# GpSimd in place of VectorE for the four combined weight blocks of the mixer, behind the scatters of the last slots

## The chip, the cores and the metric

One core of one Trainium2 chip runs the whole program. The metric is device time in microseconds of one execution: median of 3 runs 1476.76 us (1476.22 to 1486.14). The profiled execution is one of its own and took 1480.18 us, with a span of 1478.5 us from the first to the last instruction.

## The reference

Three stages follow one another on 8 sequences of 576 tokens of 512 values (4,608 tokens).

```
attention   softmax over chunks of 64 keys, 8 heads of 64
experts     logits = x @ w_gate (8 experts); a sigmoid gate lets a token keep the expert of the token before
            out[b,s] = p[e] * (relu(x[b,s] @ w1[e]) @ w2[e])          w1: 512x1024, w2: 1024x512
mixer       u  = x + (x^T @ U @ V)^T                                   rank 32 across the 576 positions
            out = u + relu(u @ w_ch1) @ w_ch2                          512 -> 2048 -> 512
```

All inputs are float32. The kernel multiplies float16 pairs (a high half and the rest) and gets float32 accuracy from three products.

## The kernel before

**Stages.** Attention takes the first 210 us. The expert stage follows, up to about 722 us: the tokens are sorted by expert, and 128 of them at a time make a slot. The mixer takes the rest, to 1478 us, and is carried by TensorE.

**A slot.** The order of all work is written out by hand, and every engine takes its instructions strictly in that order. In the round of slot `t` (loop at L1429) TensorE computes layer 1 of slot `t+2` (L907), transposes the hidden rows of slot `t+1` (L960), and computes layer 2 of slot `t` (L975). ScalarE rectifies (L952), makes high halves (L965, L869), and copies the result of layer 2 into `ysb` (L982), which has one buffer. VectorE makes the low halves (L966, L870). GpSimd then scatters the rows of `ysb` to their tokens in the DRAM tensor `yd` (L788, an indirect DMA). A scatter waits for the DMA of the write to `yd` before it. From slot 33 on (`NM - 9`, with `NM` = 42) up to two scatters of a zero tile follow the scatter of each slot (L1476), 11 in all; the last one belongs to slot 38. Rounds 36 to 41 are the last six; a round lasts 11.2 us.

**Combined weights.** The mixer's second product uses a scheme with seven block products, whose weights are sums and differences of the blocks of `w_ch2`. Half of these combined blocks are made early by GpSimd in `sums_piece` and kept in DRAM. The other four (index 2, 3, 0, 1) are made by `combine` (L1066) in the rounds 36 to 40. I call the two parts of `combine` its head and its tail. The head is one addition of 128x768 (L1072, float16 in, float32 out) and four subtractions of 128x256 (L1080), and is put at the end of rounds 36, 37, 38 and 39, behind their scatters. The tail stands at the end of the next round: ScalarE makes the high half `th` (L1075, 128x1024) from the head's result, and one subtraction of 128x1024 makes the low half `tl` (L1076). So the order at the end of a round is: scatter of the slot, scatters of zero, tail of the block before, head of the next block.

**Into the mixer.** The mixer's preparation is a list `steps`. Step 0, `load_x` for five pieces (L1205, DMAs issued by SyncE), stands in round 39 ahead of layer 2; it reads `yd`, and so stands behind the scatter of slot 38 and the last zero scatter. Steps 1 to 5, `emit_x`, stand at the start of round 40's layer 2: ScalarE makes a high half (L1236), VectorE a low half (L1230). The next steps stand inside the second layers of slots 40 and 41: `emit_t` (TensorE, L1244 and L1247), `emit_u` (L1267, L1269, L1270), `emit_sa` and `emit_sb` (GpSimd L1296, L1302, L1313, L1314; ScalarE L1299, L1306; VectorE L1230; transposing DMAs L1292 of rows `row1`, `row2`, and of `row3`, which shares its memory with `row1`). The scatter of slot 40 and the tail of block 1 stand at the end of round 40, ahead of `emit_sa`. The first mixer product (L1523) reads what these DMAs bring.

Of the kernel before, what the change touches and what calls it, by code (L numbers as in the profile page):

```python
# [13 lines left out]
ALU = mybir.AluOpType  # L14
# [26 lines left out]
def chunk_attention__moe__mixer_kernel(  # L41
# [15 lines left out]
    nc = tc.nc  # L57
# [33 lines left out]
    bh, bl = (t[:, :HC * 3 * HD].rearrange("p (c o n) -> p c o n", c=HC, o=3) for t in c2)  # L91
    b12 = [t[:, HC * 3 * HD:].bitcast(F32).rearrange("p (c n) -> p c n", n=HD) for t in c2]
# [402 lines left out]
    with tc.manual_schedule():  # L495
# [7 lines left out]
            out=tri, in_=ones, pattern=[[-1, 128]], compare_op=ALU.is_ge, fill=0.0, base=0, channel_multiplier=1  # L503
# [14 lines left out]
        for b in range(B):  # L518
# [23 lines left out]
            out=wg_l, in0=wg_raw, scalar=S_WG, in1=wg_h, op0=ALU.mult, op1=ALU.subtract  # L542
# [512 lines left out]
    th, tl = [], []  # L1055
# [10 lines left out]
    def combine(c):  # L1066
        bf, t = (
            m_p.tile([128, 512, 2], F32, tag="raw64", name="raw64").rearrange("p a b -> p (a b)") for _ in range(2)
        )
        bf = bf[:, :3 * HD].rearrange("p (o n) -> p o n", o=3)  # L1070
        t = t.rearrange("p (o n) -> p o n", o=4)
        nc.vector.tensor_tensor(out=bf, in0=bh[:, c], in1=bl[:, c], op=ALU.add)  # L1072
        sums(nc.vector, t, bf[:, 0], b12[0][:, c], bf[:, 1], bf[:, 2])
        yield
        nc.scalar.activation(out=th[c], in_=t, func=AF.Copy)  # L1075
        nc.vector.tensor_tensor(out=tl[c], in0=t, in1=th[c], op=ALU.subtract)  # L1076

    def sums(engine, t, b11, b12, b21, b22):
        for n, x, y in ((0, b12, b11), (2, b22, b12), (1, b22, t[:, 0]), (3, b21, t[:, 1])):
            engine.tensor_tensor(out=t[:, n], in0=x, in1=y, op=ALU.subtract)  # L1080
# [289 lines left out]
    with tc.manual_schedule():  # L1370
# [58 lines left out]
        for t in range(EN, NM):  # L1429
# [48 lines left out]
            if NM - 6 <= t < NM - 2:  # L1478

                combined = combine((2, 3, 0, 1)[t - NM + 6])  # L1480
                next(combined)
# [242 lines left out]
```

## Time and profile before

| quantity | value |
|---|---|
| median of 3 runs | 1476.76 us |
| profiled execution, and its span | 1480.18 us, 1478.5 us |
| TensorE matmul busy | 1355.0 us, 92% of the span |
| VectorE busy | 1086.6 us, 73% |
| ScalarE busy | 761.6 us, 52% |
| GpSimd busy | 624.9 us, 42% |
| chain that ended last, by engine | PE 58%, DVE 14%, DMA 11%, ACT 5%, issue 5%, POOL 3% |

PE is TensorE, DVE is VectorE, ACT is ScalarE, POOL is GpSimd, SP is SyncE. The shares are means over three stages with different limits. What a change in the rounds 36 to 41 is worth is to be read from the stretch of 660 to 740 us.

### The profile page before, as it was taken

The page shows a single profiled execution, that of the slowest core. Times are in us where ns is not written, and L with a number is a line of the kernel's source. Part 1 is how long each engine was busy: PE and PEld are TensorE (multiplying, and loading weights), DVE is VectorE, ACT ScalarE, POOL GpSimd, SP SyncE. Part 2 cuts the span into 40 slices and gives each one's busy share as a digit, 9 for nine tenths or more (in the row PEclk, how much of TensorE's full clock was granted, in tenths as well). Part 3 has the DMA queues.
Part 4 walks back from the last instruction along what each step waited for, and adds up shares of the span by engine and source line. Part 5 has one row for each costly group of instructions (what it writes and reads, how often), then busy time and mean ns, then how long its engine had stood idle before and what let it go on. Part 6 is the DMA issues. An engine that isn't in the chain of part 4 may idle for free.

```text
span 1478.5 us, 33713 instructions
## 1 busy us (share of the span) xinstructions
PE 1355.0 (92%) x12070; PEld 988.3 (67%) x12070; DVE 1086.6 (73%) x1740; ACT 761.6 (52%) x1158; POOL 624.9 (42%) x640
## 2 busy tenths in 40 slices
PE   7687888899999999999679999999999999999995
PEld 5676763444544544545357888888878888888884
DVE  5677767477777777767567778778778788877772
ACT  5566851466666666665344444444444444444441
POOL 2356322125767766533233334434434443443331
PEclk9889998999999999999999999999999999999998
DMA  8879873888569788532486778777788887877873
GB/s 200 210 211 213 203 181 76 269 222 205 130 187 238 175 235 252 134 76 63 138 195 123 148 151 167 159 145 165 154 164 157 158 161 137 166 147 140 141 131 83
DMA packets 513342, 244.27 MB, mean 165 GB/s; under 512 B 429652, under 2 KB 472660, under 8 KB 512916
## 3 DMA queue, kind: packets, MB, share of 16 engines
q1 hardware_dynamic: 505572, 223.14, 68.1%
q0 software_dynamic: 7600, 18.89, 4.6%
q8 instruction: 104, 1.70, 0.5%
q14 instruction: 66, 0.54, 0.1%
HBM read 163.96 MB, written 39.19 MB: 137 GB/s over the span
## 4 chain that ended last, share of the span: by engine, by line
PE 58%; DVE 14%; DMA 11%; ACT 5%; issue 5%; POOL 3%; SPq 2%; DVEq 0%; another core or an unknown queue 0%; ACTq 0%; POOLq 0%
PE y L975 14%; PE o L1585 13%; PE h L907 13%; PE a L1523 12%; DMA c<-in_q_dram 3%; POOL r L1556 3%; PE m L960 2%; DMA w1l<-c 2%; DMA w1h<-c 2%; DVE hn L1566 2%; ACT hn L1565 2%; ACT r L1552 1%; DVE pre L1548 1%; DVE pre L1551 1%; DMA hT<-hn 1%
## 5 line engine op out<-in xcount | busy, mean ns | idle before, releaser
L1556 POOL TENSOR_TENSOR r<-r 128x256 f32<-128x256 f32 x216 | 222.8, 1032 | 439.0 <-ACT r L1552 427.7
L1585 PEld LDWEIGHTS <-hT 128*128 128x128 f16 x3024 | 296.8, 98 | 52.2 <-issue 9.5
L975 PE MATMUL y<-w2h,hT 128*128 (+1 forms) x672 | 208.8, 383 | 0.1
L1566 DVE TENSOR_TENSOR hn<-r,hn 128x768 f16<-128x768 f32 (+1 forms) x144 | 171.5, 1191 | 33.7 <-ACT hn L1565 33.7
L1552 ACT ACTIVATE r<-pre 128x1024 f32<-128x1024 f32 x72 | 76.1, 1057 | 221.1 <-DVE pre L1551 221.1
L1523 PEld LDWEIGHTS <-w1h 128*128 128x128 f16 x1512 | 148.2, 99 | 47.3 <-DMA w1h<-c 17.5
L975 PEld LDWEIGHTS <-hT 128*128 128x128 f16 x1008 | 99.2, 99 | 114.2 <-issue 6.0
L1523 PEld LDWEIGHTS <-w1l 128*128 128x128 f16 x1512 | 147.0, 98 | 36.6 <-DMA w1l<-c 15.1
L1585 PE MATMUL o<-c,hT 128*128 128x256 f16 x1296 | 166.5, 274 | 4.0 <-DMA hT<-hn 3.7
L907 PE MATMUL h<-w1h,xT 128*128 (+1 forms) x624 | 166.3, 379 | 1.9 <-ACT h L952 1.9
L907 PEld LDWEIGHTS <-xT 128*128 128x128 f16 x936 | 91.5, 98 | 112.1 <-DMA xT<-xs 1.4
L1565 ACT ACTIVATE hn<-r 128x768 f16<-128x768 f32 (+1 forms) x144 | 136.6, 949 | 39.5 <-POOL r L1556 34.3
L788 POOL DMA_INDIRECT yd<-ysb,idx x39 | 61.5, 1577 | 162.6 <-ACT ysb L982 106.5
L975 PE MATMUL y<-w2l,hT 128*128 (+1 forms) x336 | 128.5, 382 | 0.0
L1523 PE MATMUL a<-c1h,w1h 128*128 128x256 f16 x576 | 114.0, 276 | 4.3 <-DMA w1h<-c 2.9
L966 DVE TENSOR_TENSOR hT<-m,hT 128x512 f16<-128x512 f32 x78 | 50.2, 687 | 88.6 <-ACT hT L965 88.6
L1523 PE MATMUL a<-c1h,w1l 128*128 128x256 f16 x576 | 112.0, 273 | 0.0
L870 DVE SCALAR_TENSOR_TENSOR w1l<-w1s,w1h 128x1024 f32 (+1 forms) x76 | 93.4, 1265 | 24.3 <-ACT w1h L869 22.6
L1585 PE MATMUL o<-w2s,hT 128*128 128x256 f16 x864 | 107.1, 274 | 0.0
L1585 PE MATMUL o<-w1s,hT 128*128 128x256 f16 x864 | 106.7, 273 | 0.0
L907 PE MATMUL h<-w1l,xT 128*128 (+1 forms) x312 | 92.8, 379 | 0.0
L870 DVE SCALAR_TENSOR_TENSOR w2l<-w2s,w2h 128x1024 f32 (+1 forms) x76 | 90.1, 1227 | 2.6 <-ACT w2h L869 1.2
(318 smaller groups left out, 2563.0 us busy)
## 6 DMA issues: line engine op xcount, KB each, us to landing
w1s<-in_moe_w_dram SPq DMA_DIRECT2D x38, 1024.0 KB
w2s<-in_moe_w_dram SPq DMA_DIRECT2D x38, 1024.0 KB
raw<-in_moe_w_ch_dram SPq DMA_DIRECT2D x32, 512.0 KB
c1h<-in_v_dram SPq DMA_DIRECT2D x144, 64.0 KB
xd<-xhl SPq DMA_DIRECT2D x36, 256.0 KB
w1l<-yd SPq DMA_DIRECT2D x28, 256.0 KB
c<-in_q_dram SPq DMA_DIRECT2D x12, 512.0 KB
c<-in_k_dram SPq DMA_DIRECT2D x12, 512.0 KB
```

Source lines behind the costliest of these rows:

```text
L788: nc.gpsimd.indirect_dma_start(out=yd, out_offset=bass.IndirectOffsetOnAxis(ap=at, axis=0), in_=y, in_offset=None, bounds_check=NT - 1, oo ...
L870: nc.vector.scalar_tensor_tensor(out=l, in0=x, scalar=scale, in1=h, op0=ALU.mult, op1=ALU.subtract)
L907: nc.tensor.matmul(out=ps[g], lhsT=x[:, a, :], rhs=w(kk, slice(g * 512, g * 512 + 512)), start=(i == 0 and j == 0), stop=(i == KD - 1 and ...
L960: nc.tensor.transpose(out=ps[g][:, a], in_=h[:, g, a], identity=ident)
L966: nc.vector.tensor_tensor(out=hT[:, g, 1], in0=ps, in1=hT[:, g, 0], op=ALU.subtract)
L975: nc.tensor.matmul(out=ps, lhsT=hT[:, f // 4, a, f % 4], rhs=w(f, slice(0, DM)), start=(i == 0 and j == 0), stop=(i == KF - 1 and j == 2),)
L1523: nc.tensor.matmul(out=out if len(z.shape) == 2 else out.rearrange("p (g n) -> p g n", n=128), lhsT=u[:, u_at(a, x, kk)], rhs=z, start=(fi ...
L1552: nc.scalar.activation(out=r[:, 0:4], in_=pre, func=AF.Relu)
L1556: nc.gpsimd.tensor_tensor(out=r[:, o], in0=r[:, x], in1=r[:, y], op=op)
L1565: nc.scalar.activation(out=row3[:, 0], in_=x, func=AF.Copy)
L1566: nc.vector.tensor_tensor(out=row3[:, 1], in0=x, in1=row3[:, 0], op=ALU.subtract)
L1585: nc.tensor.matmul(out=y if len(z.shape) == 2 else y.rearrange("p (g n) -> p g n", n=128), lhsT=hT[:, h_at(a, x, c2)], rhs=z,  start=(c == ...
```

## The change

The five instructions of the head and the subtraction of the tail are issued by GpSimd. Nothing is moved in the written order, so they stand in GpSimd's queue behind the scatters of their rounds. ScalarE's `th` stays.

```diff
@@ def combine(c):
-        nc.vector.tensor_tensor(out=bf, in0=bh[:, c], in1=bl[:, c], op=ALU.add)
-        sums(nc.vector, t, bf[:, 0], b12[0][:, c], bf[:, 1], bf[:, 2])
+        nc.gpsimd.tensor_tensor(out=bf, in0=bh[:, c], in1=bl[:, c], op=ALU.add)
+        sums(nc.gpsimd, t, bf[:, 0], b12[0][:, c], bf[:, 1], bf[:, 2])
         yield
         nc.scalar.activation(out=th[c], in_=t, func=AF.Copy)
-        nc.vector.tensor_tensor(out=tl[c], in0=t, in1=th[c], op=ALU.subtract)
+        nc.gpsimd.tensor_tensor(out=tl[c], in0=t, in1=th[c], op=ALU.subtract)
```

`sums` issues the four subtractions on the engine that it is given:

```
    def sums(engine, t, b11, b12, b21, b22):
        for n, x, y in ((0, b12, b11), (2, b22, b12), (1, b22, t[:, 0]), (3, b21, t[:, 1])):
            engine.tensor_tensor(out=t[:, n], in0=x, in1=y, op=ALU.subtract)
```

## Rows read from the trace of the kernel before

**Rows 1.** The page's first line, for the whole execution.
```profile
span 1478.5 us, 33713 instructions
```

**Rows 2.** Busy time by stretch: length, then each engine's busy us, clock, DMA.
```profile
690.00:700.00 10.00, 10.00 (x52) 5.00 (x50) 6.03 (x10) 5.35 (x8) 2.07 (x2) 1.00 0.33 103
700.00:710.00 10.00, 6.14 (x29) 3.07 (x28) 8.90 (x14) 5.71 (x10) 0.97 (x1) 0.94 0.20 69
```

**Rows 3.** The chain that ended last, 690 to 735: start us, length, what.
```profile
690.04 5.18 PE h L907 x24
...
698.12 4.54 DMA w1l<-yd
...
722.51 4.22 DMA w1h<-c
...
726.84 0.64 ACT c L1306
```

**Rows 4.** GpSimd in order of time: start us, length, instruction, [idle before, releaser].
```profile
677.12 1.71 POOL L788 DMA_INDIRECT yd<-zero,idx  x1 [2.90 <-DMA yd<-zero,idx]
...
684.56 1.86 POOL L788 DMA_INDIRECT yd<-zero,idx  x1 [2.01 <-DMA yd<-ysb,idx]
687.77 0.97 POOL L788 DMA_INDIRECT yd<-zero,idx  x1 [1.36 <-DMA yd<-zero,idx]
691.00 0.97 POOL L788 DMA_INDIRECT yd<-ysb,idx  x1 [2.25 <-ACT ysb L982]
694.01 1.10 POOL L788 DMA_INDIRECT yd<-zero,idx  x1 [2.03 <-DMA yd<-ysb,idx]
703.44 0.97 POOL L788 DMA_INDIRECT yd<-ysb,idx  x1 [8.34 <-ACT hT L965]
717.90 1.17 POOL L788 DMA_INDIRECT yd<-ysb,idx  x1 [13.49 <-ACT ysb L982]
719.66 1.42 POOL L1296 TENSOR_TENSOR w2h<-w1h 128x256 f32<-128x256 f32 x1 [0.59 <-PE y L975]
...
724.48 0.72 POOL L1314 TENSOR_TENSOR w2h<-w1h 128x256 f32<-128x256 f32 x1
```

**Rows 5.** Waits of SyncE's DMA queue, 640 to 760: total us, times, longest.
```profile
SPq L1205 <- DMA yd<-zero,idx: 5.8, 1, 5.8
```

**Rows 6.** SyncE's issues in order of time: the first loads of the mixer.
```profile
696.27 1.80 SPq L1205 DMA_DIRECT2D w1h<-yd  x4
```

**Rows 7.** ScalarE in order of time, rounds 37, 38 and 40.
```profile
679.39 1.05 ACT L1075 ACTIVATE w1s<-raw 128x1024 f16<-128x1024 f32 x1
680.34 2.16 ACT L869 ACTIVATE w1h<-w1s 128x1024 f32 x2
...
703.76 1.95 ACT L1236 ACTIVATE w1l<-w1h,psel 128x512 f16<-128x512 f32 x3
```

**Rows 8.** VectorE in order of time, at both ends of round 40.
```profile
703.91 1.22 DVE L1076 TENSOR_TENSOR w1s<-raw,w1s 128x1024 f16<-128x1024 f32 x1
705.05 0.95 DVE L1072 TENSOR_TENSOR raw<-c,c 128x768 f32<-128x768 f16 x1
...
707.51 2.73 DVE L1230 SCALAR_TENSOR_TENSOR w1l<-w1h,psel,w1l 128x512 f16<-128x512 f32 x4
...
719.27 1.22 DVE L1076 TENSOR_TENSOR w1s<-raw,w1s 128x1024 f16<-128x1024 f32 x1
```

**Rows 9.** TensorE in order of time: `emit_t`, and layer 2 behind it.
```profile
708.31 0.38 PE L1247 MATMUL m<-w1l,uA 128*96 128x512 f16 x1 [3.39 <-DVE w1l L1230]
...
712.16 0.39 PE L975 MATMUL y<-w2h,hT 128*128 x1
```

**Rows 10.** GpSimd's lines of like operations: ns min/median/max, first and last start us.
```profile
L1108 POOL TENSOR_TENSOR sums<-c,c x8: 902/905/1892, 527.8 to 606.3; 128x384 f32<-128x384 f16 x8
...
L1302 POOL TENSOR_TENSOR w2h<-w2h,w1h x12: 727/731/1052, 721.2 to 1349.7; 128x256 f32<-128x256 f32 x12
...
L590 POOL TENSOR_TENSOR w1l<-w1s,w1h x4: 2128/2132/2136, 68.1 to 104.2; 128x1024 f16<-128x1024 f32 x4
```

## The prediction

> **What bounds it now.** I read the page first, then busy time by stretch around the change, then the chain that ended last, then each engine in order of time. The span is 1478.5 us [rows 1]; the profiled execution took 1480.18 us, 3.4 us above the median of the runs, 1476.76. Up to slot 39's second layer TensorE has no gap: 10.00 of 10 us busy; in the next 10 us it is busy for 6.14 [rows 2]. So what VectorE does in rounds 36 to 38 is hidden already, and only the passage into the mixer, from about 697 to 731 us, is set by something else. The reader should see two strands in it. One is the data: the loads of the mixer's input wait for the last zero scatter [rows 5], start at 696.27 [rows 6] and land at 698.12 + 4.54 = 702.66 [rows 3]. The other is VectorE: at 703.91 it makes a tail, at 705.05 a head, and only from 707.51 the low halves [rows 8] for which TensorE has idled 3.39 us at 708.31 [rows 9]. This second strand is what the change takes off. GpSimd looks free, with 8.34 and 13.49 us of idle time ahead of the scatters of slots 39 and 40 [rows 4]; but its queue carries the scatters on which the first strand hangs, and it runs strictly in order.
>
> **Prices.** No row shows this 128x768 addition on GpSimd. The nearest, 128x384 of the same types, takes 0.905 us, at most 1.892; twice that is 1.8 to 3.8, and I take 1.8, since the median is nearly the minimum. A subtraction of 128x256 takes 0.73. So a head costs 1.8 + 4 x 0.73 = 4.7 us, against 707.51 - 705.05 = 2.5 on VectorE [rows 8]. The tail has its shape in a row: 2.13 [rows 10], against 1.22. GpSimd gets 4 x (4.7 + 2.1) = 27 us more; VectorE loses 15.
>
> **Meetings.** GpSimd's 128x256 addition at 719.66 takes 1.42 [rows 4] where its like takes 0.73: VectorE's subtraction of two SBUF operands ran until 719.27 + 1.22 = 720.49 [rows 8], and the excess is what was left of it. So where the two meet, one waits for the other. An instruction on GpSimd loses between 0 and 1.22 us by it, a VectorE instruction between 0 and 2.13 (behind a tail). The Trainium skill (SBUF — State Buffer, section "Who interferes with whom") says more: the shared ports are locked for a whole instruction, and the later engine fully blocks. This row agrees with it; with a lock the sum below is 5.5 us, with evenly shared ports it would be about 4.5.
>
> **The queue, step by step.** Four heads and four tails stand in GpSimd's order; nothing in the order of the DMAs changes, but each is issued later.
> Head 2 starts when slot 36's second zero scatter ends, 677.12 + 1.71 = 678.83, and ends at 683.6. Only then come slot 37's scatter (0.2 us of issue, 0.97) and its zeros after 2.01 and 1.36 us of DMA wait [rows 4], up to 690.1. Tail 2, with 0.7 for a meeting, and head 3 last from there to 697.8. Slot 38's scatter is issued at 698.1 instead of 691.00, so 7.1 late, and the last zero scatter, 3.01 behind it as now, at 701.1 instead of 694.01. The loads of the mixer's input start at 703.4 and land at 709.8, again 7.1 late.
> Behind the zero scatter come tail 3 (702.3 to 704.4) and head 0, with another 0.7, to 709.9. ScalarE's `th` of block 0 cannot start before it, and lasts 1.05 [rows 7]; behind it in ScalarE's order stands `emit_x`, which so starts at 711.1 instead of 703.76: 7.3 late. This is the added wait; queued behind it are all of ScalarE's high halves, and VectorE and TensorE wait for those.
> Here VectorE's relief comes back. Its low halves no longer stand behind a tail and a head; the first follows its high half by 0.7, at 711.8 instead of 707.51, 4.3 late. But tail 0 is released by the same `th` and meets them: up to 2.1 more, and I take it whole, because it is issued first. The low halves, `emit_t` and the rest of layer 2, which resumes at 712.16 now [rows 9], are then some 6 us late, and so is slot 40's scatter, 717.90 now.
> Head 1 is done by then (about 719.5 against 723.9). Tail 1 stands between that scatter and `emit_sa`: 2.1 more for L1296, less the 0.7 that it lost to VectorE's tail, so L1314 ends 6 + 1.4 = about 7 us later than 725.2 [rows 4], at 732.2. The transposition of `row1` gains the 1.2 of VectorE's tail and lands 4.8 late, at 726.73 + 4.8 = 731.5 (722.51 + 4.22 now). ScalarE's 726.84 step needs both [rows 3], and goes to 732.3: **5.5 us late.** From there the mixer has the same work, and I see nothing that gives a late start back.
>
> **What stays covered.** `th` of blocks 2 and 3 also wait for their heads. Block 2's moves from 679.39 to 683.6 and pushes ScalarE's weight halves from 680.34 to 684.6 [rows 7]; with VectorE's half they are ready by about 688, and TensorE needs them in the middle of the layer that runs from 690.04 to 695.22 [rows 3], 4.6 us later. If a head took 9.3 us, that cover would be gone. Tensor work of slot 40 is held up by 2 to 4 us through block 3's `th`, but `emit_x` comes later still, so it adds nothing.
>
> **The sum.** Without any meeting the result is 5.5 - 0.7 - 0.7 - 2.1 = 2.0 us late; with one more lock of 1.22 in each of tail 2, head 3, tail 3 and head 0 it is some 10. On the profiled execution: 1480.18 + 5.5 = 1485.7, with 1482 to 1490. On the median of the runs: 1482.3, with 1478.8 to 1486.8. About 1%, 14.8 us, is what a measurement can tell here, so this counts as no change.
>
> **Rivals.**
> *The queue absorbs it.* GpSimd has 8.34 and 13.49 us of idle time there and is busy 42% of the whole. If the loads do not hang on the late scatters, or heads cost near VectorE's 2.5, only the relief is left: the first low half follows `emit_x` at 703.76 by 0.7 + 0.7, and TensorE's 708.31 becomes about 705.1. That gives -3.2: 1473.6. Against it: SyncE's wait names the zero scatter [rows 5], and the idle time lies behind the heads, not where they stand. 0.16.
> *A lock in nearly every instruction.* Heads 2, 3 and 0 stand one behind the other on the path; each microsecond more in a head counts three times. By the worst of rows 4 and 10 a head is 3.8 + 4 x 1.42 = 9.5 and a tail 2.13 + 1.22 = 3.35. Then slot 38's scatter comes at 707.9, the loads land near 719.6, and `emit_x` starts near 726, 22 late; with the relief the end is about 20 late: 1496.8. From heads of 7.8 on the loss passes 1%. Against it: ScalarE stands still while it waits for a head, so VectorE has little to do then, and meetings should be few. 0.08. The lock of the page named above is what would make it.
> *TensorE's wait hides even the late loads*, so that the result is within 2 us of now (1475 to 1479): for it speaks that TensorE already idles there, against it that the wait is filled by the first strand from 702.66 on. It lies between the first rival and the forecast, 0.08.
>
> **Numbers.** Forecast 0.68. Its own range is 1478.8 to 1486.8. To leave out no more than 2 in 10 I go down over half of the first rival, to 1474.5, and up to 1489, which takes in the upper bound of the meetings. Faster by over 1% (under 1462) has no mechanism: 0.02. Slower by over 1% (over 1491.5) is the second rival: 0.08. The rest, 0.90, is within 1%.
>
> **What would show it.** Between slots 36 and 39 GpSimd's rows should show five additions and subtractions after each round's zero scatters, 4.7 to 5.5 us together. Slot 38's scatter should come about 7 us after where it is now, and the first L1205 loads with it. ScalarE should idle ahead of L1075 with the head's last subtraction as releaser. VectorE should have no L1072 and no L1076, and its L1230 should follow L1236 directly. TensorE's gap ahead of L1247 should be longer, not gone, and the first L1523 should start 4 to 7 us later. The prediction is wrong if the loads start near 696 in spite of the late scatters, if heads take under 3 or over 8 us, or if the mixer's own length changes: nothing in it is touched.

## The result and the profile after

The changed kernel is slower: 1492.78 us, median of four runs (1491.46 to 1496.45), against 1476.49 (1474.85 to 1486.14) for the kernel before on the same chip. The ratio is 1.010, 95% interval 1.006 to 1.014, or 9 to 21 us. The profiled executions say 1493.23 and 1480.18 us, 13.05 apart. Forecast were 5.5 us, at most 1489: the sign was right, the size was not. The kernel before ran 17 to 31 times beside each experiment, and its medians there were 1478.15 to 1480.05 us; so part of the 16.3 us between the two medians here may be the luck of four executions.

Where are the 13 us? I measure both traces from ScalarE's copy of slot 37's result (L982), the last event that the change cannot reach, to the first matmul of the mixer's second product (L1585). I call this **the passage**. First the kernel before, ScalarE and then TensorE, then the same two rows after.

```profile
678.89 0.60 ACT L982 ACTIVATE ysb<-y 128x512 f32<-128x512 f32 x1 [1.22 <-issue]
```
```profile
714.76 0.38 PE L1267 MATMUL m<-w1h,vA 128*128 128x512 f16 x1
...
726.78 0.28 PE L1523 MATMUL a<-c1h,w1h 128*128 128x256 f16 x1 [2.90 <-DMA w1h<-c]
...
756.87 2.08 PE L1585 MATMUL o<-c,hT 128*128 128x256 f16 x9 [0.29 <-issue]
```
```profile
678.35 0.60 ACT L982 ACTIVATE ysb<-y 128x512 f32<-128x512 f32 x1 [1.22 <-issue]
```
```profile
712.29 0.59 PE L1244 MATMUL m<-w1l,uA 128*128 128x512 f16 x1 [7.92 <-ACT w1l L1236]
716.14 0.59 PE L1247 MATMUL m<-w1l,uA 128*96 128x512 f16 x1 [3.26 <-DVE w1l L1230]
...
721.17 0.61 PE L975 MATMUL y<-w2h,hT 128*128 x1
...
725.75 0.38 PE L1267 MATMUL m<-w1h,vA 128*128 128x512 f16 x1
...
737.60 0.28 PE L1523 MATMUL a<-c1h,w1h 128*128 128x256 f16 x1 [2.69 <-DMA w1h<-c]
...
768.28 1.14 PE L1585 MATMUL o<-c,hT 128*128 128x256 f16 x9 [0.29 <-issue]
```

The passage went from 756.87 - 678.89 = 77.98 to 768.28 - 678.35 = 89.93 us: 11.95 longer. Ahead of it the execution after is 0.5 us shorter, behind it 1.6 longer; so nearly all of the profiled 13.05 lies here. The stretch behind it varied from 719.2 to 729.1 us over all the executions below, whatever was changed, and that is why each experiment is read by its passage as well as by its runs.

The whole page hides this. GpSimd is busy 44% of the span after:

```profile
span 1491.5 us, 33726 instructions
...
PE 1363.1 (91%) x12070; PEld 992.6 (67%) x12070; DVE 1087.9 (73%) x1716; ACT 761.1 (51%) x1158; POOL 652.2 (44%) x664
```

GpSimd in order of time says more; it answers to [rows 4]. From one slot's scatter to the next, 682.93 to 697.97, its queue needs 15.04 us, and the only idle times in it are the waits for the scatters' DMAs. A round lasted about 11.2 us before.

```profile
682.93 1.00 POOL L788 DMA_INDIRECT yd<-ysb,idx  x1 [0.15 <-issue]
685.94 0.98 POOL L788 DMA_INDIRECT yd<-zero,idx  x1 [2.01 <-DMA yd<-ysb,idx]
688.28 0.97 POOL L788 DMA_INDIRECT yd<-zero,idx  x1 [1.35 <-DMA yd<-zero,idx]
689.26 2.14 POOL L1076 TENSOR_TENSOR w1s<-raw,w1s 128x1024 f16<-128x1024 f32 x1
691.35 1.65 POOL L1072 TENSOR_TENSOR raw<-c,c 128x768 f32<-128x768 f16 x1
693.07 1.60 POOL L1080 TENSOR_TENSOR raw<-c,raw 128x256 f32<-128x256 f32 x1
694.63 1.70 POOL L1080 TENSOR_TENSOR raw<-raw,c 128x256 f32<-128x256 f32 x1
696.30 1.52 POOL L1080 TENSOR_TENSOR raw<-raw,raw 128x256 f32<-128x256 f32 x2
697.97 0.99 POOL L788 DMA_INDIRECT yd<-ysb,idx  x1 [0.15 <-issue]
...
711.78 2.16 POOL L1076 TENSOR_TENSOR w1s<-raw,w1s 128x1024 f16<-128x1024 f32 x1
713.86 1.66 POOL L1072 TENSOR_TENSOR raw<-c,c 128x768 f32<-128x768 f16 x1
715.60 1.06 POOL L1080 TENSOR_TENSOR raw<-c,raw 128x256 f32<-128x256 f32 x1
...
717.76 2.30 POOL L1080 TENSOR_TENSOR raw<-raw,raw 128x256 f32<-128x256 f32 x2
728.90 1.18 POOL L788 DMA_INDIRECT yd<-ysb,idx  x1 [8.84 <-ACT ysb L982]
```

Note the prices: in head 3 (691.35 to 697.82) two of the four subtractions take 1.60 and 1.70, though one alone takes 0.73 [rows 10]; the other two, 1.52 together, are nearly undisturbed. SyncE's wait, the row of [rows 5], is now 7.2 us, and the loads of [rows 6] start at 703.14:

```profile
703.14 1.80 SPq L1205 DMA_DIRECT2D w1h<-yd  x4
```

ScalarE, as in [rows 7]: it idles 6.36 us for head 0, and `emit_x` is right behind that `th`.

```profile
710.57 1.06 ACT L1075 ACTIVATE w1s<-raw 128x1024 f16<-128x1024 f32 x1 [6.36 <-POOL raw L1080]
711.53 2.54 ACT L1236 ACTIVATE w1l<-w1h,psel 128x512 f16<-128x512 f32 x4
```

VectorE, as in [rows 8]. The four low halves that took 2.73 us take 7.20, while GpSimd has tail 0 and then head 1 (711.78 and 713.86 above). The first of the four, shown once more by itself, takes 3.81 of them: it ends 0.56 us after the head's addition.

```profile
688.68 7.07 DVE L870 SCALAR_TENSOR_TENSOR w2l<-w2s,w2h 128x1024 f32 x2
...
708.40 1.27 DVE L966 TENSOR_TENSOR hT<-m,hT 128x512 f16<-128x512 f32 x2
...
712.27 7.20 DVE L1230 SCALAR_TENSOR_TENSOR w1l<-w1h,psel,w1l 128x512 f16<-128x512 f32 x4 [2.60 <-ACT w1l L1236]
719.40 1.20 DVE L1230 SCALAR_TENSOR_TENSOR w1l<-w1l,psel 64x512 f16<-64x512 f32 x1
```
```profile
712.27 3.81 DVE L1230 SCALAR_TENSOR_TENSOR w1l<-w1h,psel,w1l 128x512 f16<-128x512 f32 x1 [2.60 <-ACT w1l L1236]
```

The fifth low half of the kernel before, which ended at 710.89:

```profile
710.16 0.73 DVE L1230 SCALAR_TENSOR_TENSOR w1l<-w1l,psel 64x512 f16<-64x512 f32 x1
```

Last the stretches, as in [rows 2]. TensorE does 3.95 and 4.10 us of work in the two stretches from 700 to 720, and its granted clock in 710 to 720 is 0.50, the lower of its two levels (1.2 GHz); before it was 0.89 in the same stretch.

```profile
690.00:700.00 10.00, 10.00 (x52) 5.08 (x51) 5.75 (x2) 2.33 (x5) 8.66 (x7) 1.00 0.06 20
700.00:710.00 10.00, 3.95 (x21) 1.89 (x20) 9.12 (x6) 4.21 (x7) 8.83 (x7) 0.91 0.40 125
710.00:720.00 10.00, 4.10 (x8) 1.07 (x7) 7.73 (x5) 4.12 (x6) 9.59 (x8) 0.50 0.07 26
```

Lateness against the kernel before, both counted from the L982 copy, in us:

| event | forecast | measured |
|---|---|---|
| slot 38's scatter | 7.1 | 7.5 |
| first loads (L1205) | 7.1 | 7.4 |
| `emit_x` on ScalarE | 7.3 | 8.3 |
| last low half of `emit_x` done | about 6 | 10.25 |
| layer 2 resumes (L975) | 6 | 9.55 |
| slot 40's scatter | 6 | 11.5 |
| first mixer matmul (L1523) | 5.5 | 11.4 |
| first matmul of the second product (L1585) | 5.5 | 11.95 |

The queue was forecast within half a microsecond as far as the loads. The rest is lost between `emit_x` and slot 40's scatter.

### The profile page after: what moved, and what is told of

Read it like the earlier page. It is cut to its first block, busy times and chain, and to the rows that moved or that the text cites. A ratio compares the mean times of both kernels' runs of the same rounds, so it can differ in the third digit from the quotient of the medians.

```text
span 1491.5 us, 33726 instructions
## 1 busy us (share of the span) xinstructions
PE 1363.1 (91%) x12070; PEld 992.6 (67%) x12070; DVE 1087.9 (73%) x1716; ACT 761.1 (51%) x1158; POOL 652.2 (44%) x664
## 4 chain that ended last, share of the span: by engine, by line
PE 47%; DVE 15%; issue 10%; DMA 10%; POOL 9%; ACT 5%; SPq 3%; POOLq 0%; DVEq 0%; ACTq 0%
PE o L1585 13%; PE a L1523 13%; PE y L975 9%; PE h L907 7%; DMA c<-in_q_dram 4%; POOL r L1556 2%; DMA w1h<-c 2%; DVE hn L1566 2%; DMA w1l<-c 2%; ACT hn L1565 2%; ACT r L1552 1%; PE m L960 1%; POOL yd L788 1%; DVE pre L1548 1%; POOL xs L330 1%
## 5 line engine op out<-in xcount | busy, mean ns | idle before, releaser
L1585 PEld LDWEIGHTS <-hT 128*128 128x128 f16 x3024 | 296.3, 98 | 50.8 <-issue 9.3
L975 PE MATMUL y<-w2h,hT 128*128 (+1 forms) x672 | 210.3, 385 | 0.0
L1523 PEld LDWEIGHTS <-w1h 128*128 128x128 f16 x1512 | 149.6, 100 | 46.9 <-DMA w1h<-c 16.7
L975 PEld LDWEIGHTS <-hT 128*128 128x128 f16 x1008 | 99.8, 99 | 115.8 <-issue 8.6
L1523 PEld LDWEIGHTS <-w1l 128*128 128x128 f16 x1512 | 148.3, 99 | 37.7 <-DMA w1l<-c 14.6
L1585 PE MATMUL o<-c,hT 128*128 128x256 f16 x1296 | 165.6, 273 | 3.5 <-DMA hT<-hn 3.2
L975 PE MATMUL y<-w2l,hT 128*128 (+1 forms) x336 | 129.2, 385 | 0.0
L966 DVE TENSOR_TENSOR hT<-m,hT 128x512 f16<-128x512 f32 x78 | 50.2, 686 | 92.7 <-ACT hT L965 92.7
L1523 PE MATMUL a<-c1h,w1h 128*128 128x256 f16 x576 | 114.2, 276 | 2.8 <-DMA w1h<-c 2.7
L870 DVE SCALAR_TENSOR_TENSOR w1l<-w1s,w1h 128x1024 f32 (+1 forms) x76 | 91.6, 1240 | 31.2 <-ACT w1h L869 30.1
L1523 PE MATMUL a<-c1h,w1l 128*128 128x256 f16 x576 | 113.9, 276 | 0.0
L1585 PE MATMUL o<-w2s,hT 128*128 128x256 f16 x864 | 107.3, 274 | 0.0
L1585 PE MATMUL o<-w1s,hT 128*128 128x256 f16 x864 | 106.1, 273 | 0.0
L870 DVE SCALAR_TENSOR_TENSOR w2l<-w2s,w2h 128x1024 f32 (+1 forms) x76 | 100.3, 1361 | 2.0 <-ACT w2h L869 1.2
```

The source lines that it names most:

```text
L870: nc.vector.scalar_tensor_tensor(out=l, in0=x, scalar=scale, in1=h, op0=ALU.mult, op1=ALU.subtract)
L966: nc.vector.tensor_tensor(out=hT[:, g, 1], in0=ps, in1=hT[:, g, 0], op=ALU.subtract)
L975: nc.tensor.matmul(out=ps, lhsT=hT[:, f // 4, a, f % 4], rhs=w(f, slice(0, DM)), start=(i == 0 and j == 0), stop=(i == KF - 1 and j == 2),)
L1523: nc.tensor.matmul(out=out if len(z.shape) == 2 else out.rearrange("p (g n) -> p g n", n=128), lhsT=u[:, u_at(a, x, kk)], rhs=z, start=(fi ...
L1585: nc.tensor.matmul(out=y if len(z.shape) == 2 else y.rearrange("p (g n) -> p g n", n=128), lhsT=hT[:, h_at(a, x, c2)], rhs=z,  start=(c == ...
```

## The experiments

The theory after the result: (a) GpSimd's occupied queue makes the scatters, and with them the loads, late; (b) head 1, not only tail 0, takes turns with the low halves; (c) the longer gap of TensorE costs clock behind it. The rivals: one of these alone is the whole loss, or the late start of the loads is not on the path. Experiments 1 to 5 and 7 edit the changed kernel; 6 and 8 the kernel before; 9 is built on 6.

**1 and 2. Half of the change each.** Only blocks 2 and 3 on GpSimd, or only blocks 0 and 1.

```diff
+        eng = nc.gpsimd if c in (2, 3) else nc.vector     # experiment 2: (0, 1)
-        nc.gpsimd.tensor_tensor(out=bf, in0=bh[:, c], in1=bl[:, c], op=ALU.add)
-        sums(nc.gpsimd, t, bf[:, 0], b12[0][:, c], bf[:, 1], bf[:, 2])
+        eng.tensor_tensor(out=bf, in0=bh[:, c], in1=bl[:, c], op=ALU.add)
+        sums(eng, t, bf[:, 0], b12[0][:, c], bf[:, 1], bf[:, 2])
...
-        nc.gpsimd.tensor_tensor(out=tl[c], in0=t, in1=th[c], op=ALU.subtract)
+        eng.tensor_tensor(out=tl[c], in0=t, in1=th[c], op=ALU.subtract)
```

> Blocks 2 and 3 on GpSimd, blocks 0 and 1 on VectorE as before. Theory: the loss of the change (16.3 us by the medians, 13 by the profiled executions) has three parts. The queue: slot 38's scatter and the mixer's loads come 7 us late because GpSimd needs more per round than the round lasts. The meetings in round 40: tail 0 and head 1 on GpSimd slow VectorE's low halves of emit_x. The clock: TensorE runs at half speed some 4 us longer after the longer gap. Here the first part stays whole: scatter of slot 38 near 698, loads starting near 703 and landing near 709.5. The second is gone, since VectorE makes tail 0 and head 1 while it waits for the loads: the four low halves of emit_x take 2.7 us instead of 7.2. So +3 to +6 us against before. Rival (the loss lies in rounds 36 to 39, where ScalarE and VectorE are slowed by the heads, in proportion to their number): +7 to +9.

Measured for blocks 2 and 3: 1490.14 against 1480.05, ratio 1.0072 (1.0050 to 1.0094), passage 8.76 us longer than before. That is the rival's figure, but not by the rival's cause: `emit_x`'s low halves run at full speed (2.73), and something else is late. One row of VectorE and one of TensorE, with line numbers one higher than in the changed kernel:

```profile
705.52 0.42 DVE L1081 TENSOR_TENSOR raw<-c,raw 128x256 f32<-128x256 f32 x1 [6.08 <-POOL w1s L1077]
```
```profile
707.73 1.97 PE L960 MATMUL m<-ident,h 128*128 128x128 f32 x8 [6.72 <-DVE hT L966]
```

Head 0, on VectorE again, waits 6.08 us for GpSimd's tail 3, since both use the buffers of tag `raw64`; slot 40's hidden rows stand behind it on VectorE, and TensorE waits 6.72 us for them. My expectation missed this: two engines that share a buffer pair brought in a wait that neither kernel has. What the run does show is that the late loads come with blocks 2 and 3 (scatter 38 at 698.61, loads at 704.50).

> Blocks 0 and 1 on GpSimd, blocks 2 and 3 on VectorE as before. Theory: slot 38's scatter and the loads come as before (691 and 696.3), since no head stands ahead of them; emit_x starts near 704; its low halves meet tail 0 and head 1 and take about 7 instead of 2.7 us, which eats the relief of 3.7 on VectorE; tail 1 stands ahead of emit_sa for 2 us. So +1 to +5 us. Rival (loss in proportion to the number of heads): +7 to +9.

Measured for blocks 0 and 1: 1485.96, ratio 1.0029 (1.0001 to 1.0057), passage 1.96 longer. GpSimd's and VectorE's rows:

```profile
688.74 0.97 POOL L788 DMA_INDIRECT yd<-ysb,idx  x1 [2.26 <-ACT ysb L982]
```
```profile
702.26 7.34 DVE L1231 SCALAR_TENSOR_TENSOR w1l<-w1h,psel,w1l 128x512 f16<-128x512 f32 x4 [0.75 <-ACT w1l L1237]
```

The scatter is on time (12.10 us after the L982 copy, 12.11 before), and so are the loads (693.89), and the low halves still take 7.34. So the 4.6 us of turns with tail 0 and head 1 arise without the late loads, and without them most is paid by the tail and head that VectorE no longer has. The theory's 1 to 5 held in the passage and in the ratio.

**3. The zero scatters earlier**, three in a round, so that none stands between the last heads.

```diff
-                for at in range(NM + 2 * (t - NM + 9), min(NM + 2 * (t - NM + 10), NS)):
+                for at in range(NM + 3 * (t - NM + 9), min(NM + 3 * (t - NM + 10), NS)):
```

> The changed kernel (all four blocks on GpSimd), with three zero scatters per round instead of two, so that the last one belongs to round 36 and no longer stands with its DMA wait between the heads. Theory: GpSimd's work per round then fits into the round, slot 38's scatter comes near 692 instead of 698, the loads start by 696 instead of 703, emit_x near 704 to 706 instead of 711.5. What is left are the meetings in round 40, tail 1 and a part of the clock: +2 to +7 us against before, so 9 to 14 faster than the changed kernel. Rival (the heads cost by meeting VectorE in rounds 36 to 39, the scatters' order does not matter): within 4 us of the changed kernel.

Measured: 1487.96, ratio 1.0062 (1.0028 to 1.0095), passage 9.09 longer; a miss of the theory's 2 to 7, and within the rival's 4 us of the changed kernel in the passage. The zeros only moved: with three in a round they hold up the queue up to round 36, head 2 starts 3.7 us later there, and the queue still takes 11.6 us from slot 37's scatter to slot 38's:

```profile
685.55 0.99 POOL L788 DMA_INDIRECT yd<-ysb,idx  x1 [0.15 <-issue]
...
697.16 0.99 POOL L788 DMA_INDIRECT yd<-ysb,idx  x1 [0.16 <-issue]
```

Slot 38's scatter comes 0.9 us earlier than in the changed kernel and the loads 3.3; the passage gains 2.9. The tail and the head alone nearly fill a round, 10.4 of 11.2 us; two subtractions took 3.38 us, where 1.46 is the price without meetings.

**4. GpSimd as occupied, but not reading.** Tail 0 and head 1 become fills that write and read nothing; the low half of block 0 and all of block 1 are left out of the result.

```diff
+        if c == 1:
+            for _ in range(5):
+                nc.gpsimd.memset(whole, 0.0)
+            nc.gpsimd.memset(t, 0.0)
...
+        if c == 0:
+            for _ in range(2):
+                nc.gpsimd.memset(tl[c].bitcast(F32), 0.0)
```

> The changed kernel, but tail 0 and head 1 are replaced by fills with zeros of about the same total length (6.8 us), which read nothing from SBUF; so the low half of block 0 and all of block 1 are not computed. Theory (VectorE's two-operand instructions and GpSimd's reading instructions take turns): scatters and loads are as late as in the changed kernel (loads at 703), but the four low halves of emit_x take 2.7 to 3.2 us instead of 7.2, emit_t ends near 717 instead of 721.2, and the time is 3 to 7 us under the changed kernel. Rival (GpSimd's occupied queue alone makes the loss, whatever it does): no change against the changed kernel, low halves still near 7 us.

Measured: 1488.16, ratio 1.0055 (1.0031 to 1.0078); the passage is 6.88 us shorter than the changed kernel's. The loads are as late as there. VectorE, then GpSimd (line numbers ten higher):

```profile
716.65 2.74 DVE L1240 SCALAR_TENSOR_TENSOR w1l<-w1h,psel,w1l 128x512 f16<-128x512 f32 x4 [2.60 <-ACT w1l L1246]
719.30 0.74 DVE L1240 SCALAR_TENSOR_TENSOR w1l<-w1l,psel 64x512 f16<-64x512 f32 x1
```
```profile
717.21 4.99 POOL L1075 MEMSET raw<- 128x1024 f32 x5
```

GpSimd is busy all through the four low halves (the two fills for tail 0 start at 716.13), and they take 2.74 us. So it is not GpSimd's being busy but its reading that stretches them. 4.9 us come back directly (8.33 to 3.39), and 2.0 more behind them, 1.7 of it in the mixer's first blocks; experiment 5 names that part. No run takes tail 0 or head 1 away alone.

**5. The clock held up.** The changed kernel with idle matmuls in TensorE's gaps.

```diff
+        idle(33, keep_ps[0], c1h[:, 0, :512])     # ahead of emit_t(0)
...
+        if 1 <= m < 5 and keep_ps:
+            idle(2, keep_ps[0], c1h[:, 0, :512])
...
+        if m == 0 and keep_ps:
+            idle(15, keep_ps[0], c1h[:, 0, :512])
```

> The changed kernel, with dummy matmuls in TensorE's gaps ahead of and inside emit_t (33 ahead of it, 15 behind its first matmul, 2 ahead of each later pair), so that the engine is not idle there. I measure the passage, from ScalarE's copy of slot 37's result to the first matmul of the mixer's second product: 78.0 us before, 89.9 with the change. Theory (some 2 us of the loss are half speed: 12 matmuls of layer 2 behind emit_t take 4.6 us instead of 2.6): the granted clock stays 1.00 up to 726 us, and the passage is 2 to 2.5 us shorter, 87.4 to 87.9. Rival (the clock costs nothing, since VectorE sets the pace there): 89.5 to 90.5.

One stretch of the changed kernel, then of this one, where the twelve matmuls of layer 2 stand:

```profile
720.00:724.00 4.00, 3.99 (x10) 1.22 (x10) 1.77 (x3) 2.49 (x3) 0.05 (x1) 0.50 0.00 0
```
```profile
720.00:724.00 4.00, 3.22 (x16) 1.40 (x16) 2.19 (x4) 2.49 (x3) 0.00 (x0) 1.00 0.00 0
```

The clock stays at 1.00 up to 732 us and the passage is 3.24 us shorter than the changed kernel's; the low halves take 7.21 us, as in that kernel. 1.56 us come back ahead of the mixer, where the twelve matmuls take 2.60 us instead of 4.58. The rest comes back in the mixer's first blocks, where 24 matmuls behind a wait (L1523) take 2.81 us instead of 4.51. So the lower clock is a cost of its own, in all above the 2 to 2.5 expected. But the 24 matmuls take 4.16 us in the kernel before too, so that part is hardly a loss of the change. In the runs' times it does not appear: 1492.9, ratio 1.0113 (1.0076 to 1.0150).

**7. Occupation against meetings in the queue.** Heads and tails of blocks 2 and 3 become fills; these blocks are not computed.

```diff
+        if c in (2, 3):
+            for _ in range(4):
+                nc.gpsimd.memset(whole, 0.0)
+            nc.gpsimd.memset(t, 0.0)
...
+        if c in (2, 3):
+            for _ in range(4):
+                nc.gpsimd.memset(tl[c].bitcast(F32), 0.0)
```

> The changed kernel, but heads and tails of blocks 2 and 3 on GpSimd are fills of about the same length as these have without a meeting (4.8 and 2.2 us); so these two blocks are not computed. It splits the 7.4 us by which slot 38's scatter and the loads are late into occupation and meetings. Theory: the queue is overfull even without meetings (13.3 us of scatters, DMA waits, tail and head in a round of 11.2), so slot 38's scatter stays 4 to 5.5 us late, the passage 2 to 3.5 us shorter than 89.9. Rival (only meetings make the queue late): the scatter is less than 2 us late and the passage 6 to 7 us shorter.

Measured: 1489.0, ratio 1.0067 (1.0042 to 1.0092); the passage is 3.70 us shorter than the changed kernel's, a little more than the 2 to 3.5 expected.

```profile
681.39 0.97 POOL L788 DMA_INDIRECT yd<-ysb,idx  x1 [0.16 <-issue]
...
694.96 0.97 POOL L788 DMA_INDIRECT yd<-ysb,idx  x1 [0.16 <-issue]
```

Slot 38's scatter is 4.9 us later than before, against 7.5 in the changed kernel: about 4.9 us of its lateness are occupation of an in-order queue, 2.6 are meetings. Without any meeting the queue still needs 694.96 - 681.39 = 13.57 us in a round of 11.2.

**6 and 8. The relief without GpSimd.** If tail 0 and head 1 must not stand ahead of the low halves, they can move on VectorE itself. In 8 they go behind `emit_x`'s low halves. In 6, tail 3 and head 0 go into the middle of round 38, tail 0 and head 1 to its end, and tail 1 behind `emit_x`. Here the edit of 6; that of 8 has the same form:

```diff
+                if t == NM - 4:
+                    next(combined, None)
+                    combined = combine(0)
+                    next(combined)
...
             if t == NM - 2:
                 step(5)
+                next(combined, None)
...
-            next(combined, None)
-            if NM - 6 <= t < NM - 2:
+            if t <= NM - 4:
+                next(combined, None)
+            if NM - 6 <= t <= NM - 4:
-                combined = combine((2, 3, 0, 1)[t - NM + 6])
+                combined = combine((2, 3, 1)[t - NM + 6])
```

> The kernel before, all on VectorE, with only tail 0 and head 1 moved behind emit_x's low halves in round 40. It prices the relief that the change gives alone. Theory: 3.2 us or more off TensorE's gap at 708.3, of which some comes back because VectorE's head then stands ahead of L1255: the passage 2 to 4 us shorter than 78.0, time 0.1 to 0.3% under the kernel before. Rival: no change of the passage.

Measured for 8: 1478.57, ratio 0.9996 (0.9974 to 1.0018), passage 2.59 us shorter than before. `emit_t` follows its low half by 0.17 where TensorE waited 3.39 [rows 9], but the next step of `emit_u` now waits for L1255, behind head 1:

```profile
704.06 0.38 PE L1247 MATMUL m<-w1l,uA 128*96 128x512 f16 x1 [0.17 <-DVE w1l L1230]
...
711.01 0.38 PE L1267 MATMUL m<-w1h,vA 128*128 128x512 f16 x1 [1.24 <-DVE w1h L1255]
```

> The kernel before, all on VectorE, with another order: tail 3 and head 0 in the middle of round 38, tail 0 and head 1 at its end, tail 1 behind emit_x in round 40. Theory: what VectorE's share of this work really costs is that tail 0 and head 1 stand ahead of emit_x's low halves and tail 1 ahead of those of emit_sa. Without them emit_x's first low half starts near 703.5 instead of 707.5, TensorE's gap of 3.4 us ahead of L1247 goes, and with it most of the half-speed time behind it. The passage is 4 to 6.5 us shorter than 78.0, and the time 0.2 to 0.45% under the kernel before. Rival (the loads and ScalarE's order set emit_t, VectorE's place does not matter): within 1 us of 78.0.

Measured for 6: 1477.07 against 1478.15, ratio 0.9986 (0.9961 to 1.0010), passage 6.45 us shorter than before. TensorE's row (the copy of L982 is at 675.87):

```profile
747.40 2.08 PE L1591 MATMUL o<-c,hT 128*128 128x256 f16 x9 [0.29 <-issue]
```

It was run again on another chip:

> The earlier order on VectorE once more, since its passage was 6.4 us shorter than before while its runs gave only 0.9986 (0.9961 to 1.001) of the kernel before, where 6.4 us would be 0.9956. Theory (the passage's gain is in the time, hidden by the spread of the runs): 0.994 to 0.998, with an upper end of the interval below 1. Rival (the rest of the kernel gives the gain back): 0.998 to 1.001 again, with the stretch behind the passage some 3 to 5 us longer than the 721.6 us of the kernel before.

1475.38 against 1478.24, ratio 0.9979 (0.9956 to 1.0002), passage 5.74 us shorter. Both point estimates lie below 1, by 1.1 and 2.9 us; neither interval excludes 1. The stretch behind the passage took 722.08 us in this profiled execution and 724.31 in that of experiment 6, against 721.60 in the kernel before, so the rival's 3 to 5 us more did not come here. So the stall that the change aimed at was worth some 6 us of passage, and could be had without GpSimd; how much of it reaches the end is not settled.

**9. Experiment 6 with idle matmuls**, 13 ahead of a mixer bank and 11 inside `emit_t(9)`; the 11 overwrite part of the mixer's sums.

```diff
+        if m == 9:
+            idle(11, spare_ps[0], c1h[:, 0, :512])
...
+            if j == 0 and q == 0:
+                idle(13, spare_ps[0], c1h[:, 0, :512])
```

> The kernel with the earlier order on VectorE (its passage: 71.5 us), plus dummy matmuls in two of TensorE's gaps: 13 while the mixer's third bank waits for the transposed row3, 11 inside emit_t of the ninth piece, where 2.6 us are spent on a low half. Theory (the gaps let the clock fall, and the work behind them pays for it: the first mixer block takes 4.2 us where 24 matmuls at full clock take 2.6, the first nine matmuls of the second product 2.08 instead of 1.14): the passage is 1 to 1.5 us shorter than 71.5, the time about 0.45 to 0.65% under the kernel before. Rival (VectorE and the DMAs set the pace there, the clock is free): passage 71 to 72, and the time as with the earlier order alone.

Measured: 1478.52, ratio 0.9996 (0.9973 to 1.0019), passage 72.15 us against 71.53 in experiment 6: nothing gained. Only one of the two gaps was filled. The wait of 2.6 us belongs to the piece of 64 rows ahead of the second product (L1598), and is still there; the 11 matmuls (L137) run 22 us behind that product's first matmul:

```profile
751.01 0.58 PE L1251 MATMUL m<-w1l,uA 64*96 64x512 f16 x1 [2.63 <-DVE w1l L1230]
...
774.10 2.54 PE L137 MATMUL o<-c1h,ident 128*128 128x512 f16 x11
```

The 13 did their work: the 24 matmuls behind them take 2.78 us instead of 4.15. But the dip of the clock only moved, to 732 and later:

```profile
736.00:740.00 4.00, 4.00 (x21) 2.83 (x20) 2.60 (x5) 0.28 (x1) 0.00 (x0) 0.50 0.67 125
```

So the rival's figure came out with the first gap filled, and nothing was learnt of the second.

## Why the prediction was wrong

**What was right.** The mechanism: GpSimd's queue is in order, the mixer's loads hang on its last zero scatter, and head 0 holds up `th` and `emit_x`. Scatter and loads were 7.5 and 7.4 us late against 7.1; experiment 2, with blocks 2 and 3 back on VectorE, brings them back on time. That they came so close is partly luck: counted from the L982 copy, head 2 started 1.3 us earlier than I had taken it (677.02, behind a shorter zero scatter), and took 1.1 us longer. The covers held too: TensorE was busy for 10.00 us from 690 to 700.

**Prices, a little low.** Heads took 5.8 to 6.5 us, and I gave 4.7 to 5.4: the addition cost 1.65 instead of the 1.8 taken, but in heads 3 and 0 two subtractions met VectorE and lost 0.9 to 1.0 each, where I allowed 0.7 for a tail and a head together. With that `emit_x` came 8.3 late instead of 7.3: **1.0 us.**

**The step that failed: "Head 1 is done by then".** I let tail 0 alone meet the low halves, 2.1 us taken whole, and checked only that head 1 ended before slot 40's scatter. It did, and that was the wrong test: head 1 runs beside the low halves and stops them too. From the first to the end of the last the five took 712.27 to 720.60 = 8.33 us, against 3.38 before and 5.5 forecast: **2.85 us.** Experiment 4 shows the cause: with fills in their place they take 3.39. My bound was wrong too: I let a VectorE instruction lose at most 2.13 us, behind one instruction of GpSimd's. The first low half (712.27 to 716.08) outlasted two, the tail up to 713.94 and the addition up to 715.52. By these rows, an estimate, tail 0 cost 1.7 of the 4.95 us and head 1 the other 3.3.

**The missing term: the clock.** I moved `emit_t` and the rest of layer 2 by the same 6 us at an unchanged length, and gave no reason. TensorE's gap grew (idle for 7.92 and 3.26 us, where it had been 0.45 and 3.39), its granted clock was at the lower level, 0.50, from 712 to 724, and the same twelve matmuls of layer 2 took 721.17 to 725.75 = 4.58 us instead of 712.16 to 714.76 = 2.60: **2.0 us.** Experiment 5, with these matmuls at 2.60 again, gave 1.56 us back ahead of the mixer.

Forecast 5.5 + 1.0 + 2.85 + 2.0 = 11.35, against 11.4 measured at the mixer's start and 11.95 at the second product. That it closes so well is partly luck, since two deviations of 0.3 us cancel in it. One of them: the transposition of `row1` did not gain the 1.2 us of VectorE's tail, because beside tail 1 the two low halves ahead of it took 3.48 us instead of 2.08.

**The rivals.** The time came out where I had put the second rival, over 1491.5. That the queue absorbs it, or that TensorE's wait hides the late loads, was wrong: the relief on VectorE was real (no tail and head there), but was spent on the turns and on a queue that runs late. The lock in nearly every instruction was right as a mechanism and mis-sized: I priced it into the heads (9.5 us), where it added 1 to 2, and not into the low halves, where it added 5. Its chance was too small: that ScalarE stands still and VectorE has little to do was argued and not read from a row, and L870, two operands in SBUF, stood beside tail 2 and head 3 for 7.07 us.

**What stays open.** Late loads and a late `th` of block 0 reach `emit_x` within 2 us of each other, and no run took one away alone in the changed kernel. By ScalarE's row `th` came last. From the start of the loads to `emit_x` it is 8.4 us there and 6.5 in experiments 6 and 8, where no `th` stands ahead of it; so, by estimate, the loads had landed at least 1.8 us earlier, and head 0 behind the late scatters set the path. The medians differ by 16.3 us, the passages by 11.95; the rest lies within the spread of the stretch behind, whose cause I did not find. That spread may also be why the gains of experiments 5 and 6 in the passage are not, or only partly, seen in the runs' times; no run separates it from a gain that is given back later.

## What to carry to other kernels

Before work is put into an in-order queue, add up the queue's demand for a round, DMA waits included, and compare it with the round (here 13.6 to 15 us in 11.2); the engine's busy share (42%) says nothing of it. Where two engines take turns, price every instruction of either side that overlaps the other's work on the path, both ways, and do not take one wait each for granted: here one instruction outlasted two of the other engine's. And a gap that grows on TensorE may be paid for a second time, in the clock of the work behind it.

## What the runs showed of the hardware

Where both had work that reads SBUF, one waited for the other, but not strictly in turns. Tail 0 and the addition of head 1 followed each other at their usual lengths (2.16 and 1.66), and the low half that had started during the tail ended behind both (3.81 us, against 0.74 for one in the kernel before). Beside the four subtractions behind them the other low halves took 1.20 each, and the subtractions 1.05 to 1.17 instead of 0.73. In head 3, beside L870, two subtractions took 1.6 to 1.7. The first L870 there started, by its record, 0.58 us ahead of tail 2 (688.68 and 689.26), and still the tail took its usual 2.14, and the L870 5.40. The two L870, two operands in SBUF, took 7.07 us after and 2.36 before, where GpSimd had only the rest of a scatter; L966, one operand in PSUM, took 1.27 and 1.28. VectorE's rows of before:

```profile
686.62 1.28 DVE L966 TENSOR_TENSOR hT<-m,hT 128x512 f16<-128x512 f32 x2
688.00 2.36 DVE L870 SCALAR_TENSOR_TENSOR w2l<-w2s,w2h 128x1024 f32 x2
```

GpSimd's fills cost VectorE nothing (2.74 for the four low halves). The Trainium skill (SBUF — State Buffer, section "Who interferes with whom") states that a VectorE instruction with both inputs in SBUF contends with a GpSimd instruction that reads SBUF, and not with one that only writes it. The rows agree: L870 and the low halves meet tails and heads (7.07, 7.20), and the fills meet nothing. L966, with one input in SBUF, was not held up beside head 0 either (1.27). The lock that the prediction took from that section, under which the later engine waits for a whole instruction, agrees with the low half that started in tail 0; it does not agree with the L870 that started ahead of tail 2 and ended behind it.
